# One bank, one copy for two pairs of f tiles, and eight 64-row products in one stay: the first MLP layer of an FNet block

## The chip, the core and the metric

The kernel runs on one core of a Trainium2 chip. A core has a matrix engine (TensorE; PE in the profile, its weight loads PEld), a vector engine (DVE), a scalar engine (ACT), GpSimd (POOL) and a queue engine (SP) that here only issues transfers. Each takes its instructions in the order written into the program. Matmuls write PSUM, eight banks of 128 partitions by 512 fp32; DVE and ACT copy from there to SBUF. The metric is the time of one execution on the device in microseconds: the median of three runs before the change is 1242.02 (1241.27 to 1242.12).

## The reference, cut to what matters

x is 2048 tokens by 576 features; w1 is 576x4608, w2 is 4608x576.

```python
xn = _layernorm(x)
a = einsum("bsd,ed->bse", xn, dft_hid_re); b = einsum("bsd,ed->bse", xn, dft_hid_im)
y = einsum("ts,bse->bte", dft_seq_re, a) - einsum("ts,bse->bte", dft_seq_im, b)
h = maximum(einsum("bsd,df->bsf", xn, w1), 0)
return x + y + einsum("bsf,fd->bsd", h, w2)
```

## The kernel before, in words

**Numbers.** Every operand is split into a high and a low float16 part, and a product of two operands is three matmuls: high by high, high by low, low by high. Most products are those of a scheme with seven half-size products in place of eight (`PRODUCTS` for the second layer and the sequence DFT, `P1` to `P7` for the first layer).

**The loops.** The 4608 hidden features are nine blocks b of 512, and the tokens four groups g of 512. A *step* is one (b, g). In it the first layer makes the hidden values `h` of this step, and the second layer (`mlp2`, seven products m0 to m6 of twelve matmuls 128x288 each) works on the `h` of the step before. After the 36 steps come the hidden DFT (`dft1`) and the sequence DFT.

**The first layer from block 2 on** (`BB = 2`, 28 steps; blocks 0 and 1 do it with whole products in `mlp1_step`). A block has two *pairs* of f tiles of 128 (index i). For each pair `pair_products` makes seven products P1, P2, P6, P5, P7, P3, P4 on 256 tokens: six matmuls 128x256 each (two blocks of 128 features, three matmuls for each), written into half of a bank (256 columns of 512). 576 features are four blocks of 128 and a *rest* of 64. The rest enters with four of the products (`REST`): each has two more matmuls, one with the high weights and one with the low weights. In the 128 rows of both operands the 64 rest rows stand twice: in the weights the same rows again, in the tokens (`xT[g][:, KM]`) high and then low part. So the matmul with the low weights adds low by high and, with its other 64 rows, low by low. A pair's step is thus 50 matmuls, both pairs' 100.

**Banks and copies.** Four banks: one `u` for each pair, and `v`, `w` for both. P1 is copied out of `u` (ACT), then P6 adds onto it in PSUM, is copied (ACT), then P7 (DVE), then P4. P2 goes to `v`; P5 and then P3 to `w`. Each product that adds onto a bank must wait until the copy before has read it. The copies and the arithmetic on the values (`free`, `use`, `end_s`) are 128x256 for each pair. At the end `end_hi` (ACT) and `end_lo` (DVE), 128x1024 each, make high and low part of the four sums S1 to S4 of a pair; they stand in the list `ends`, which later places in the order take from.

**The order of the work** is written by hand: the list of `(do, q)` from L1075 on. In it `first` and `second` issue the products of the two pairs, `m` the second layer's, `later1` and `later2` the arithmetic on values, `ready` and `brief` one piece each of the preparation of the next block (loads, maxima, scales, `split_w1b`, `sums_w1`, `split_w2`), `t_sum` sums of token operands, and `count` one piece of the sequence DFT's scales: `sum_c` sums a loaded 128x1024 tile `f` on ACT (L1027), then `first_c` asks for the next one over SP (L1020) into the same buffer. So each `f` has the time from one `count` to the next to land, and ACT stands until it has. There are two `count`s a step.

**What m0 to m6 need.** Two PSUM tiles serve them. m0, m2, m4, m6 add onto one place, m1 has one for itself, m3 and m5 share the third; m0, m2, m3, m6 are copied out by ACT (L612), m1, m4, m5 merged by DVE (L616), and m1, m4, m5, m6 are then added to memory by a POOL transfer (`spill`, L619). m3 takes the buffer that m1 leaves, and m6 adds onto what m4's merge has read.

**64-row matmuls** stand already in `mlp1_step` (L371) and `dft1` (L1203): there the low products of the rest use only 64 rows each, in turns rows 0 to 63 and rows 64 to 127 of the array; for the second kind `xT[g][:, NKX]` holds the high part in rows 64 to 127.

The launch lays the inputs out on the host.

Of the kernel before, what the change touches and what calls it, by code (L numbers as in the profile page):

```python
# [9 lines left out]
F16 = mybir.dt.float16  # L10
# [8 lines left out]
P = 128  # L19
S = 2048  # L20
D = 576
# [28 lines left out]
def kernel(  # L50
# [35 lines left out]
    accs = [accp.tile([P, TG, D], F32, name=f"acc{g}") for g in range(NG)]  # L86
# [6 lines left out]
    raws = {}  # L93

# [9 lines left out]
    def load_w1(b, i, parts=1):  # L104
        pool, tag = (raw, "raw") if b else (mlp, "stage")
        r = raws["w1", b, i] = pool.tile([P, 2 * KT, P], F32, tag=tag, name=f"raw_w1_{b}_{i}")
# [271 lines left out]

    def mlp1_out(b, g, i, pa, pb, after=None, last=None, late=False):
# [5 lines left out]
        h = hs[b, g, i] = mlp.tile([P, 2, 7, GH], F16, tag="h", name=f"h{b}_{g}_{i}", bufs=4)  # L385
        st = mlp.tile([P, 5, GH], F32, tag="stage", name=f"s{b}_{g}_{i}")
# [5 lines left out]
        for q, src in ((slice(A11, A11 + 1), a11), (slice(A12, A22 + 1), pb)):  # L392
            hi, lo = (h[:, n, q].rearrange("p a b -> p (a b)") for n in range(2))
            with behind(after):
                order["hi"] = nc.scalar.activation(hi, src, AF.Relu).ins
                order["hl"] = stt(lo, src, 0.0, hi, ALU.max, ALU.subtract).ins  # L396
# [33 lines left out]
    flat = [a.rearrange("p a b -> p (a b)") for a in accs]  # L430
    XS = 4 * 2 * (KM // 2) * GH // 2
    xsums = [
        f[:, : XS].bitcast(F16).rearrange("p (q n k t) -> p q n k t", q=4, n=2, t=GH)
        for f in flat
    ]
    cbufs = [f[:, XS :] for f in flat]
# [59 lines left out]
    banks1, ends, gates = [], [], {}  # L496

    def freed(i, key="free"):

        order[key] = i.ins  # L500

    def pair_products(b, g, i):

        if not banks1:
            banks1.extend(ps1.tile([P, G], F32, tag="ps1", name=f"bank{k}")[:, :GH] for k in range(4))
        h = hs[b, g, i] = mlp.tile([P, 2, 7, GH], F16, tag="h", name=f"h{b}_{g}_{i}", bufs=4)
        st = mlp.tile([P, 5, GH], F32, tag="stage", name=f"s{b}_{g}_{i}")
        r21, s1, s2, s3, s4 = (st[:, n] for n in range(5))
# [4 lines left out]
        def product(n):  # L513
            ps = {P2: v, P5: w, P3: w}.get(n, u)
            first = n in (P1, P2, P5)
            x, ws, a = right(g, n), w1s[b, i], LEFT[n]
            todo = [
                (ws[:, y, a + k], x[z][:, k]) for k in range(2) for y, z in ((1, 0), (0, 0), (0, 1))
            ]
            if n in REST:  # L520
                k, c = REST[n]
                todo += [(ws[:, y, k], xT[g][:, KM, (H1, H2)[c]]) for y in range(2)]
            for m, (l, r) in enumerate(todo):
                nc.tensor.matmul(  # L524
                    ps, l, r, start=first and m == 0, stop=m == len(todo) - 1,
                    skip_group_check=not first,
                )
# [6 lines left out]
        def end_s():  # L534
# [3 lines left out]
            stt(s4, u, 0.0, s2, ALU.max, ALU.subtract)  # L538

        hi_s, lo_s = (h[:, k, S1 : S4 + 1] for k in range(2))  # L540

        def end_hi():
            order["s"] = nc.scalar.activation(hi_s, st[:, 1:], AF.Copy).ins  # L543

        def end_lo():
            order["lo"] = nc.vector.tensor_tensor(lo_s, st[:, 1:], hi_s, ALU.subtract).ins  # L546

# [4 lines left out]
            P6: lambda: freed(nc.scalar.activation(s1, u, AF.Copy)),  # L552
            P5: lambda: freed(nc.scalar.activation(c22, w, AF.Copy)),
            P7: lambda: freed(tt(c22, u, c22, ALU.add), "vfree"),  # L554
            P3: lambda: freed(tt(r21, w, s1, ALU.add), "vfree"),
# [4 lines left out]
            P3: lambda: nc.scalar.activation(r21, r21, AF.Relu),  # L560
            P4: lambda: (value(A12, u), end_s(), ends.extend((end_hi, end_lo))),
        }

        def run(n, used=False):
            if used:
                return use[n]()
            product(n)
            if n in free:
                free[n]()

        return run
# [109 lines left out]
    def sum_w2(b, i, after=("root", 4)):  # L681
# [3 lines left out]
        if b:  # L685
            junk = mlp.tile([P, 5, GH], F32, tag="stage", name=f"j{b}_{i}")
            junk = junk.rearrange("p a b -> p (a b)")[:, : 4 * EH]
            junk = junk.rearrange("p (q e) -> p q e", e=EH)
        else:
            new_w2(b, i)  # L690
            junk = w2s[b, i][:, 0, :4]
# [41 lines left out]
    def split_w2(b, i, c):  # L733
        if b and c == 0:
            new_w2(b, i)
# [247 lines left out]
    def split_d(j, c):  # L983
        k = PARTS_D[c]
        split(dsp[j][:, 0, k], dsp[j][:, 1, k], raws["d", j][:, k], sc["d"][:, j : j + 1])
# [52 lines left out]
    for n in range(2, len(steps)):  # L1038
# [26 lines left out]
        if b >= BB:  # L1065
            first, second = (pair_products(b, g, i) for i in range(NQ))
            later1, later2 = (lambda q, f=f: f(q, True) for f in (first, second))
# [6 lines left out]
            t_sum = lambda q: next(tq, None)  # L1074
            for do, q in (  # L1075
                (first, P1), (first, P2), (m, 0), (left, 0), (end, 0), (first, P6),
                (brief, 1), (first, P5), (end, 0), (later1, P2), (m, 1), (left, 1),
                (t_sum, 0), (ready, 1), (second, P1), (first, P7), (ready, 1), (m, 2),
                (second, P2), (t_sum, 0), (count, 0), (brief, 1), (first, P3), (first, P4), (later1, P7), (m, 3),
                (second, P6), (later1, P3), (later1, P4), (later2, P2), (brief, 1), (m, 4),  # L1080
                (t_sum, 0), (second, P5), (ready, 1), (m, 5), (end, 0), (second, P7),
                (t_sum, 0), (end, 0), (brief, 1), (m, 6), (count, 0), (brief, 2),
                (second, P3), (second, P4), (later2, P7), (later2, P3), (later2, P4), (brief, 1),
            ):
                do(q)
# [304 lines left out]
```

## Time and profile before

| what | value |
|---|---|
| median of three runs | 1242.02 us |
| profiled execution, first to last instruction | 1239.7 us |
| PE busy | 1226.7 us (99%), 10269 matmuls |
| DVE busy | 1006.8 us (81%), 1919 instructions |
| ACT busy | 704.1 us (57%), 1192 instructions |
| POOL busy | 159.9 us (13%) |
| TensorE clock granted | 1.000 |
| stretch of the 28 steps with `pair_products` | 192.4 to 788.1 us |

The profile's own execution has a span of 1239.7 us, 2.3 us under the median of the runs, which time the launch and the end as well. Busy time of PE is an envelope: matmuls overlap in the pipeline, a row's mean duration (273 ns for 256 columns) is the latency of one, and the distance from one start to the next is shorter. A line such as `L524 PE MATMUL bank<-acc,w1buf 128*128 128x256 f16 x768` names line, engine, operation, output and inputs, the array's rows and columns in use, the output's shape, and the count; then come busy time and mean ns, then the engine's idle time just before and what ended it.

### The profile page before, as it was taken

Reading aid. Unit: us, or ns where it says so; the run is one execution under the profiler, and the core shown is the slowest. Engines: PE = TensorE matmul, PEld = TensorE weight load, DVE = VectorE, ACT = ScalarE, POOL = GpSimd, SP = SyncE. Lnnn points to the kernel's source line nnn. Section 1 sums busy time; section 2 is a strip of 40 time slices with the busy share of each in tenths; the row PEclk is TensorE's granted clock in tenths of the full one; section 3 lists DMA queues with packets and bytes.
Section 4 is the critical chain, followed back from the end, with each engine's and each line's share of the span. In section 5 each row is a group of like instructions: output and inputs, shape, how many; then the busy total and the mean of one; then the engine's idle time right before and its main releaser. Section 6 shows DMA issues by size and latency. Waiting matters only on the chain.

```text
span 1239.7 us, 25267 instructions
## 1 busy us (share of the span) xinstructions
PE 1226.7 (99%) x10269; PEld 980.6 (79%) x10269; DVE 1006.8 (81%) x1919; ACT 704.1 (57%) x1192; POOL 159.9 (13%) x208
## 2 busy tenths in 40 slices
PE   8999999999999999999999999999999999999998
PEld 7656657888888888888888888777777777777776
DVE  8999999878778788788787788466887878787875
ACT  5655566666676776766766666445543333333332
POOL 2432212121111112121212111200000000000000
PEclk9999999999999999999999999999999999999999
DMA  8995537556666766676676766720054344434420
GB/s 313 210 163 97 85 68 153 127 119 151 140 136 141 137 143 121 135 140 137 112 172 122 158 141 123 127 71 1 1 174 141 122 125 138 142 120 129 134 88 20
DMA packets 80324, 157.28 MB, mean 127 GB/s; under 512 B 22224, under 2 KB 41168, under 8 KB 80208
## 3 DMA queue, kind: packets, MB, share of 16 engines
q1 hardware_dynamic: 57424, 113.20, 28.7%
q0 software_dynamic: 22784, 42.48, 25.8%
q8 instruction: 80, 1.31, 0.4%
q14 instruction: 36, 0.29, 0.1%
HBM read 104.53 MB, written 51.90 MB: 126 GB/s over the span
## 4 chain that ended last, share of the span: by engine, by line
PE 92%; DVE 5%; ACT 1%; issue 1%; DMA 0%; SPq 0%; ACTq 0%; DVEq 0%
PE p L601 28%; PE p L1322 27%; PE bank L524 23%; PE pd L1193 8%; PE p L346 5%; DVE w2s L186 1%; DVE st L209 1%; DMA acc<-in_x_dram 0%; PE pd L1203 0%; DVE h L413 0%; DVE dbuf L260 0%; ACT f L1027 0%; DVE w1buf L186 0%; ACT h L543 0%; DVE h L396 0%
## 5 line engine op out<-in xcount | busy, mean ns | idle before, releaser
L601 PE MATMUL p<-w2s,h 128*128 128x288 f16 x3024 | 408.0, 286 | 1.5 <-DVE acc L616 0.8
L601 PEld LDWEIGHTS <-h 128*128 128x128 f16 x3024 | 295.6, 98 | 76.9 <-issue 1.7
L1322 PE MATMUL p<-R,cs 128*128 128x288 f16 x2688 | 329.4, 286 | 0.0
L1322 PEld LDWEIGHTS <-cs 128*128 128x128 f16 x2688 | 263.0, 98 | 66.3
L185 ACT ACTIVATE cs<-c,sc_c 128x1024 f16<-128x1024 f32 x112 | 125.2, 1144 | 196.7 <-DVE c L1255 72.3
L186 DVE SCALAR_TENSOR_TENSOR cs<-c,sc_c,cs 128x1024 f16<-128x1024 f32 x112 | 141.0, 1281 | 54.7 <-ACT cs L185 54.7
L524 PEld LDWEIGHTS <-w1buf 128*128 128x128 f16 x1600 | 156.6, 98 | 21.9 <-issue 0.7
L524 PEld LDWEIGHTS <-dbuf 128*128 128x128 f16 x1200 | 117.4, 98 | 16.1 <-issue 0.3
L524 PE MATMUL bank<-xT,w1buf 128*128 128x256 f16 x832 | 109.9, 273 | 0.0
L1193 PE MATMUL pd<-dbuf,xT 128*128 128x288 f16 x832 | 103.8, 286 | 0.0
L524 PE MATMUL bank<-acc,w1buf 128*128 128x256 f16 x768 | 102.3, 273 | 0.4 <-ACT acc L550 0.2
L546 DVE TENSOR_TENSOR h<-s,h 128x1024 f16<-128x1024 f32 x56 | 68.5, 1223 | 38.4 <-ACT h L543 38.4
L1193 PEld LDWEIGHTS <-xT 128*128 128x128 f16 x832 | 80.8, 98 | 22.0 <-issue 1.9
L619 POOL DMA_DIRECT2D spill<-dbuf x70 | 60.5, 865 | 252.7 <-DVE dbuf L616 229.7
L531 ACT ACTIVATE h<-acc 128x256 f16<-128x256 f32 x112 | 45.8, 411 | 67.3 <-DVE acc L554 66.5
L524 PE MATMUL bank<-xT,dbuf 128*128 128x256 f16 x624 | 82.3, 273 | 0.0
L543 ACT ACTIVATE h<-s 128x1024 f16<-128x1024 f32 x56 | 59.1, 1056 | 33.8 <-DVE s L538 33.5
L524 PE MATMUL bank<-acc,dbuf 128*128 128x256 f16 x576 | 76.6, 273 | 0.1
L1328 DVE SCALAR_TENSOR_TENSOR o<-p,us_c,o 128x288 f32<-128x288 f32 x112 | 57.5, 513 | 12.7 <-PE p L1322 12.0
L612 ACT ACTIVATE dbuf<-p,c_ub 128x576 f32<-128x576 f32 x70 | 51.4, 734 | 26.4 <-PE p L601 26.3
L1027 ACT ACTIVATE f<-f 128x1024 f32<-128x1024 f32 x60 | 62.8, 1046 | 0.3 <-DMA f<-in_cre_dram 0.3
L619 POOL DMA_DIRECT2D spill<-sum x42 | 36.9, 878 | 196.1 <-DVE sum L616 173.4
(164 smaller groups left out, 1529.4 us busy)
## 6 DMA issues: line engine op xcount, KB each, us to landing
spill<-dbuf POOLq DMA_DIRECT2D x70, 288.0 KB, 5.0
c<-in_cre_dram SPq DMA_DIRECT2D x32, 512.0 KB, 4.1
c<-in_cim_dram SPq DMA_DIRECT2D x32, 512.0 KB, 5.0
f<-in_cre_dram SPq DMA_DIRECT2D x30, 512.0 KB, 6.0
f<-in_cim_dram SPq DMA_DIRECT2D x30, 512.0 KB, 5.7
spill<-sum POOLq DMA_DIRECT2D x42, 288.0 KB, 4.4
raw_w<-in_w_dram SPq DMA_DIRECT2D x17, 640.0 KB, 5.2
raw_w<-in_w_dram SPq DMA_DIRECT2D x18, 576.0 KB, 4.9
```

The costliest lines, as they stand in the source:

```text
L185: nc.scalar.activation(hi, src, AF.Copy, scale=s).ins,
L186: nc.vector.scalar_tensor_tensor(lo, src, s, hi, ALU.mult, ALU.subtract).ins,
L346: order["m1"] = nc.tensor.matmul(ps[:, cols], w1s[b, i // 2][:, hl, i % 2 * KT + k], xT[g][:, kx, cols], start=(start and n == 0), stop=(s ...
L524: nc.tensor.matmul(ps, l, r, start=first and m == 0, stop=m == len(todo) - 1, skip_group_check=not first,)
L543: order["s"] = nc.scalar.activation(hi_s, st[:, 1:], AF.Copy).ins
L546: order["lo"] = nc.vector.tensor_tensor(lo_s, st[:, 1:], hi_s, ALU.subtract).ins
L601: order["pe"] = nc.tensor.matmul(ps[:, c], h[:, x, qa, c * P : (c + 1) * P], w[:, y, qb], start=first and i == 0 and j == 0, stop=i == NQ ...
L619: nc.gpsimd.dma_start(spill[g, row, col], o, accum_op=ALU.add)
L1027: nc.scalar.activation(f, f, AF.Abs, scale=2.0**-10, accum_out=sums_c[:, n, q : q + 1])
L1193: nc.tensor.matmul(ps[j], xT[g][:, kx, c * P : (c + 1) * P], dsp[j][:, hl, k], start=(t % 2 == 0 and n == 0), stop=(t % 2 == 1 and n == le ...
L1322: nc.tensor.matmul(ps, w[:, a, k], r[:, c, rq], start=first and k == 0 and j == 0, stop=k == HK - 1 and j == 2, skip_group_check=not first,)
L1328: order["o"] = nc.vector.scalar_tensor_tensor(o, ps, us["c"][:, n : n + 1], o, ALU.mult, ALU.add).ins
```

## The change

From block 2 on, `step_products(n)` replaces the two `pair_products`.

- **Shared banks.** `u` is one bank for both pairs, each in its half; `v` likewise; P5 and P3 use `w`, which is in turn bank 2 and bank 3 from step to step. A product is issued for pair 0 and then pair 1, and then one copy of 128x512 reads both. `h` is one tile for both pairs, `stage` one tile for the whole kernel, and the four `acc` tiles become one (`acct`) so that `cbufs` are two buffers of 128x512. P4 is now copied out by ACT (`s4`), and A12 and S4 are made from that copy.
- **Rest.** P2, P5, P3 and P4 keep their matmul with the high weights. The eight matmuls with the low weights (four products, two pairs) are taken out and become 64-row matmuls that stand together in `rests`, between m3 and P3: P4's and P3's of this step, and P2's and P5's of the *next* step (they open the next step's `v` and `w`). They go in turns to rows 0 to 63 and 64 to 127 of the array. The low by low part of the rest is no longer added. The first of the 28 steps does its P2 and P5 lows in the old way, and the last has only four in `rests`.
- **Order.** The list of `(do, q)` is new: P1, P5, m0, P6, P2, m1, P7, m2, m3, `rests`, P3, m4, P4, m5, m6. The two `count`s come after m2 and after m5.
- **Smaller edits.** `end_hi` and `end_lo` cover two sums of both pairs, still 128x1024, and two of them follow each of m0 and m1 in the tail. `split_w1b` and `split_d` are queued behind the latest copies out of the banks. `sum_w2` writes its unused result into the `w2s` tile of the next block, not into a `stage` buffer.

```diff
-    accs = [accp.tile([P, TG, D], F32, name=f"acc{g}") for g in range(NG)]
+    acct = accp.tile([P, NG, TG, D], F32, name="acc")
+    accs = [acct[:, g] for g in range(NG)]
...
+    stage = mlp.tile([P, 5, NQ, GH], F32, name="stage", bufs=1)
...
+    def new_h(b, g, i):
+        if i == 0:
+            h = mlp.tile([P, 2, 7, NQ, GH], F16, tag="h", name=f"h{b}_{g}")
+            for j in range(NQ):
+                hs[b, g, j] = h[:, :, :, j]
+            hs[b, g] = h
+        return hs[b, g, i]
...
-    def pair_products(b, g, i):
+    def step_products(n):
+        b, g = steps[n]
...
-        u, v, w = banks1[i], banks1[2], banks1[3]
-        c11, c22 = cbufs[i], cbufs[2]
+        u, v, w = banks1[0], banks1[1], banks1[2 + n % 2]
+        c11, c22 = cbufs
...
+        def product(q):
+            ps = {P2: v, P5: w, P3: w}.get(q, u)
+            x, a = right(g, q), LEFT[q]
+            first = q in (P1, P2, P5) and (n, q) not in begun
+            for i in range(NQ):
+                ws = w1s[b, i]
+                todo = [
+                    (ws[:, y, a + k], x[z][:, k]) for k in range(2) for y, z in ((1, 0), (0, 0), (0, 1))
+                ]
+                if q in REST:
+                    k, c = REST[q]
+                    lows = q in (P2, P5) and (n, q) not in begun
+                    todo += [(ws[:, y, k], xT[g][:, KM, (H1, H2)[c]]) for y in range(1 + lows)]
+                for m, (l, r) in enumerate(todo):
+                    nc.tensor.matmul(
+                        ps[:, i], l, r, start=first and i == m == 0,
+                        stop=m == len(todo) - 1, skip_group_check=not first or i > 0,
+                    )
+
+        def rests(also=None):
+            todo = []
+            if also is not None:
+                b2, g2 = steps[also]
+                for i in range(NQ):
+                    todo += [(banks1[1], b2, g2, i, P2, i == 0), (banks1[2 + also % 2], b2, g2, i, P5, i == 0)]
+                begun.update(((also, P2), (also, P5)))
+            for i in range(NQ):
+                todo += [(u, b, g, i, P4, False), (w, b, g, i, P3, False)]
+            for m, (ps, b_, g_, i, q, start) in enumerate(todo):
+                r, kx = m % 2, (KM, NKX)[m % 2]
+                rows = slice(r * REM, (r + 1) * REM)
+                k, c = REST[q]
+                nc.tensor.matmul(
+                    ps[:, i], w1s[b_, i][rows, 1, k], xT[g_][rows, kx, (H1, H2)[c]],
+                    start=start, stop=True, skip_group_check=not start,
+                )
...
+        def end_hi(i):
+            with behind("free"):
+                order["s"] = nc.scalar.activation(h[:, 0, S1 + 2 * i :][:, :2], stage[:, 1 + 2 * i :][:, :2], AF.Copy).ins
...
+        def sums_h():
+            nc.scalar.activation(r21, r21, AF.Relu)
             stt(s3, c11, 0.0, r21, ALU.max, ALU.subtract)
             stt(s1, c22, 0.0, r21, ALU.max, ALU.add)
             stt(s2, c22, 0.0, s3, ALU.max, ALU.subtract)
...
+        def last():
+            hi, lo = h[:, 0, A12], h[:, 1, A12]
+            nc.scalar.activation(hi, s4, AF.Copy)
+            tt(lo, s4, hi, ALU.subtract)
+            tt(s4, s4, s2, ALU.subtract)
+            for i in range(NQ):
+                ends.extend((lambda i=i: end_hi(i), lambda i=i: end_lo(i)))
...
+            P4: lambda: freed(nc.scalar.activation(s4, u, AF.Relu)),
...
-        split(w[:, 0, k], w[:, 1, k], src, sc["w1", b][:, i : i + 1])
+        with behind("free"), behind("vfree"):
+            split(w[:, 0, k], w[:, 1, k], src, sc["w1", b][:, i : i + 1])
...
+        new_w2(b, i)
+        junk = w2s[b, i][:, 0, :4]
...
             for do, q in (
-                (first, P1), (first, P2), (m, 0), (left, 0), (end, 0), (first, P6),
-                (brief, 1), (first, P5), (end, 0), (later1, P2), (m, 1), (left, 1),
-                (t_sum, 0), (ready, 1), (second, P1), (first, P7), (ready, 1), (m, 2),
-                (second, P2), (t_sum, 0), (count, 0), (brief, 1), (first, P3), (first, P4), (later1, P7), (m, 3),
-                (second, P6), (later1, P3), (later1, P4), (later2, P2), (brief, 1), (m, 4),
-                (t_sum, 0), (second, P5), (ready, 1), (m, 5), (end, 0), (second, P7),
-                (t_sum, 0), (end, 0), (brief, 1), (m, 6), (count, 0), (brief, 2),
-                (second, P3), (second, P4), (later2, P7), (later2, P3), (later2, P4), (brief, 1),
+                (run, P1), (left, 0), (run, P5), (end, 0), (end, 0), (m, 0), (brief, 1), (left, 1),
+                (run, P6), (end, 0), (end, 0), (run, P2), (t_sum, 0), (m, 1), (used, P2), (ready, 1),
+                (run, P7), (t_sum, 0), (ready, 1), (m, 2), (used, P7), (count, 0), (m, 3), (brief, 1),
+                (rest, 0), (run, P3), (brief, 1), (m, 4), (used, P3), (t_sum, 0), (ready, 1),
+                (run, P4), (used, P4), (t_sum, 0), (m, 5), (ready, 1), (count, 0),
+                (m, 6), (brief, 3),
             ):
...
-        if ends:
-            ends.pop(0)()
+        for _ in range(2):
+            if ends:
+                ends.pop(0)()
```

More of the change, by code (lines that the diff above doesn't have):

```diff
@@ L391, in mlp1_out @@
             nc.scalar.activation(r21, a21, AF.Relu)
-        for q, src in ((slice(A11, A11 + 1), a11), (slice(A12, A22 + 1), pb)):
-            hi, lo = (h[:, n, q].rearrange("p a b -> p (a b)") for n in range(2))
+        both = pb.rearrange("p (a t) -> p a t", t=GH)
+        for q, src in ((A11, a11), (slice(A12, A22 + 1), both)):
+            hi, lo = (h[:, n, q] for n in range(2))
             with behind(after):
@@ L537, in end_s @@
             stt(s2, c22, 0.0, s3, ALU.max, ALU.subtract)
[L538 to L546, printed above, removed]
+        def last():
[3 more added lines that the diff above has]
+            tt(s4, s4, s2, ALU.subtract)
+            for i in range(NQ):
+                ends.extend((lambda i=i: end_hi(i), lambda i=i: end_lo(i)))
         free = {
@@ L1065 @@
         if b >= BB:
-            first, second = (pair_products(b, g, i) for i in range(NQ))
-            later1, later2 = (lambda q, f=f: f(q, True) for f in (first, second))
+            run, rests = step_products(n)
+            used = lambda q: run(q, True)
             m = lambda q: mlp2(pb, pg, q)
```

87 lines of the change are left out of this document (41 added, 46 removed).

## The prediction

> **What bounds the kernel now.** First the page's engine totals, its clock row and the chain that ended last.
>
> ```profile
> PE 1226.7 (99%) x10269; PEld 980.6 (79%) x10269; DVE 1006.8 (81%) x1919; ACT 704.1 (57%) x1192; POOL 159.9 (13%) x208
> ...
> PEclk9999999999999999999999999999999999999999
> ...
> PE 92%; DVE 5%; ACT 1%; issue 1%; DMA 0%; SPq 0%; ACTq 0%; DVEq 0%
> PE p L601 28%; PE p L1322 27%; PE bank L524 23%; PE pd L1193 8%; PE p L346 5%; DVE w2s L186 1%; DVE st L209 1%; DMA acc<-in_x_dram 0%; PE pd L1203 0%; DVE h L413 0%; DVE dbuf L260 0%; ACT f L1027 0%; DVE w1buf L186 0%; ACT h L543 0%; DVE h L396 0%
> ```
>
> PE is the bound at full clock. Only fewer PE slots or fewer PE waits shorten the time; DVE and ACT count where they keep PE waiting. Then the busy times of the stretch of the 28 changed steps and of one step in it.
>
> ```profile
> 192.00:795.00 603.00, 601.87 (x5211) 509.47 (x5210) 489.67 (x1076) 408.69 (x800) 106.43 (x136) 1.00 0.66 137
> 384.80:406.03 21.23, 21.23 (x187) 18.02 (x186) 18.05 (x40) 13.97 (x29) 3.82 (x6) 1.00 0.65 132
> ```
>
> Columns after the length: PE, PEld, DVE, ACT, POOL. A step is 21.23 us without a gap; in all 603 us PE lacks 603.00 - 601.87 = 1.13 us. So nothing is to be had from waits: at most 1.1. But DVE has 18.05 of 21.23 us, so a merge that is wanted earlier may come late.
>
> **The low products.** From PE's timeline, slots of full-height matmuls and three places where 64-row ones stand already.
>
> ```profile
> 387.81 1.47 PE L524 MATMUL bank<-acc,w1buf 128*128 128x256 f16 x12
> 389.12 0.38 PE L524 MATMUL bank<-xT,w1buf 128*128 128x256 f16 x2
> 389.34 1.63 PE L601 MATMUL p<-w2s,h 128*128 128x288 f16 x12
> 390.81 0.82 PE L524 MATMUL bank<-xT,w1buf 128*128 128x256 f16 x6
> ...
> 392.12 1.63 PE L601 MATMUL p<-w2s,h 128*128 128x288 f16 x12
> 393.59 1.91 PE L524 MATMUL bank<-xT,w1buf 128*128 128x256 f16 x16
> ...
> 396.21 1.02 PE L601 MATMUL p<-w2s,h 128*128 128x288 f16 x7
> ...
> 804.23 1.27 PE L1193 MATMUL pd<-dbuf,xT 128*128 128x288 f16 x9
> 805.43 0.67 PE L1203 MATMUL pd<-dbuf,xT 64*128 64x288 f16 x8
> 806.02 0.79 PE L1193 MATMUL pd<-dbuf,xT 128*128 128x288 f16 x5
> ...
> 109.78 0.61 PE L371 MATMUL p<-xT,dbuf 64*128 64x512 f16 x4
> 110.31 1.04 PE L346 MATMUL p<-xT,dbuf 128*128 128x512 f16 x4
> ```
>
> Slot of 256 columns: (389.12 - 387.81) / 12 = 0.109 us. Of 288: (390.81 - 389.34) / 12 = 0.1225. A stay of eight 64-row matmuls: nine full ones from 804.23 would hand over at 804.23 + 9 x 0.1225 = 805.33; the stay begins at 805.43 (0.10 late) and lasts 0.59, where eight in turn would need 0.98 and four pairs side by side 0.49. So they run in pairs, and a stay costs about 0.10 going in and 0.10 coming out; 0.21 with the two next starts (from the starts of single matmuls). L371 agrees: 0.53 for four of 512 columns, two slots of 0.216 and 0.10.
>
> A middle step: eight slots go (0.874), four slots and a stay come (0.437 + 0.21 = 0.65): -0.224. Of 28 steps 26 are such: -5.83. The first keeps four lows in full slots: +0.21. The last has two pair slots in place of eight: -0.44. Sum A = **-6.06**.
>
> The Trainium skill ("TensorE: Matmul & The Clock Gate", section Part 3: Packing small matmuls) puts a pack at one matmul and about 4 ns more for each tile, with no price for the stay. By it a step would save 0.42 us, 28 some 11.8, and the run would take 1230. Its sister page ("TensorEngine Tiling (Array Packing)", Key Properties) says that changing the tiling mode drains the engine; the 0.21 us above agree, and the sum goes by the row.
>
> **The copies.** These are the forms that change or that stand in the way (mean ns in the middle).
>
> ```profile
> L395 ACT ACTIVATE h<-p 128x512 f16<-128x512 f32 x16 | 9.4, 591 | 18.1 <-PE p L346 17.8 <-DVE h L396 0.3
> L396 DVE SCALAR_TENSOR_TENSOR h<-p,h 128x512 f16<-128x512 f32 x16 | 10.8, 678 | 0.0
> L531 ACT ACTIVATE h<-bank 128x256 f16<-128x256 f32 x56 | 20.7, 370 | 0.2 <-PE bank L524 0.2
> L551 DVE TENSOR_TENSOR acc<-bank,acc 128x256 f32<-128x256 f32 x56 | 23.3, 416 | 3.1 <-PE bank L524 3.1
> L543 ACT ACTIVATE h<-s 128x1024 f16<-128x1024 f32 x56 | 59.1, 1056 | 33.8 <-DVE s L538 33.5
> L546 DVE TENSOR_TENSOR h<-s,h 128x1024 f16<-128x1024 f32 x56 | 68.5, 1223 | 38.4 <-ACT h L543 38.4
> L612 ACT ACTIVATE dbuf<-p,c_ub 128x576 f32<-128x576 f32 x70 | 51.4, 734 | 26.4 <-PE p L601 26.3
> L616 DVE SCALAR_TENSOR_TENSOR dbuf<-p,c_ub,dbuf 128x576 f32<-128x576 f32 x56 | 45.4, 812 | 6.5 <-PE p L601 6.1
> L185 ACT ACTIVATE w1buf<-raw_w,c_sw 128x640 f16<-128x640 f32 x20 | 16.3, 824 | 4.7 <-DVE c_sw L127 3.6 <-DVE raw_w L678 1.0
> L1027 ACT ACTIVATE f<-f 128x1024 f32<-128x1024 f32 x60 | 62.8, 1046 | 0.3 <-DMA f<-in_cre_dram 0.3
> ```
>
> Ten DVE instructions of 0.416 for each pair become ten of 0.68 for both: 1.5 us a step less by durations. ACT has seven of 0.37 to 0.41 for each pair and gets eight of about 0.6: 0.6 less. Both stay beside PE and earn nothing; the bound is 0 to -1.13, and the waits there are now are booked below.
>
> What PE has to wait for, in its new order (P1 1.31, P5 1.53, m0 1.47, P6 1.31, P2 1.53, m1 1.47, P7 1.31, m2 1.47, m3 1.47, rests 0.65, P3 1.53, m4 1.47, P4 1.53, m5 1.47, m6 1.47; sum 21.0):
> - P6 after P1's copy (ACT): 1.53 + 1.47 = 3.0 us for 0.59. P7 after P6's: the same. Next P1 after P4's copy: 2.9.
> - P4's lows after P7's add (DVE, 0.68): 2.94 and two pair slots, 3.2.
> - m3 after m1's merge (DVE, 0.81): 1.31 + 1.47 = **2.78**, where the rows above give 396.21 - 390.81 = 5.40 today. m6 after m4's merge: 1.53 + 1.47 = 3.0.
> - m2 after the sums' low part: 5.7 and more, easy.
>
> How late a merge is today, in the same step:
>
> ```profile
> 391.98 0.81 DVE L616 SCALAR_TENSOR_TENSOR sum<-p,c_ub,sum 128x576 f32<-128x576 f32 x1
> ```
>
> m1's merge ends at 392.79, 1.98 after m1's slots. In 2.78 that fits, with 0.8 over. By the order of the built program I added up a plain step of the changed kernel in the same way: DVE reaches P2's add at 8.7 us of the step (splits and sums of w1 to 5.3, S's two low parts 1.22 each, the second after ACT's at 7.45), ends m1's merge at 10.2 against m3 at 11.4, and P7's add, behind a split of 0.88, at 12.5 against 13.1. So a plain step has 1.2 and 0.6 us over: no wait.
>
> New waits, where that fails:
> - First of the 28 steps: ahead of P7's add DVE has P2's add, four sums of token operands, m1's merge, A11's low part and a w2 split, some 6.8 us where PE needs 6.05: 0.7.
> - Last step: the DFT scale is known 3.0 us into it, then ACT splits 1.0 and 0.77, then copies P1 (0.6): 5.2 against P6 at 4.3: 0.9.
> - Tail: S's parts now all follow m0's copy: 0.7 + 1.06 on ACT against m1's 1.47: 0.3.
> - Steps of blocks 0 and 1: their arithmetic is reordered among itself by a few instructions, PE's order is the same: 0 to 0.6, taken 0.3.
> - Late `f`. ACT comes to the second `count` some 4.5 us after the first has asked for its `f` (first `count` ends at 14.4 of the step, P4's copy at 18.9). If `f` is not there, ACT stands, and behind it A12's high part, then on DVE its low part, the weights' scale (a POOL reduction and three small instructions), ACT's split, DVE's sums, P2's add and m1's merge. That chain has the 1.2 us over. So PE waits when `f` takes more than about 5.7 us.
>
> How long `f` takes, over all 60, and for the one asked for at 385.1 (by the second `count` today) and at 395.9 (by the first):
>
> ```profile
> DMA to landing us min/median/max: 3.3/5.8/8.4
> ...
> L1020 SPq DMA_DIRECT2D f<-in_cre_dram x1: 327/327/327, 385.1 to 385.1; - x1
> ...
> DMA to landing us min/median/max: 7.0/7.0/7.0
> ...
> L1020 SPq DMA_DIRECT2D f<-in_cim_dram x1: 328/328/328, 395.9 to 395.9; - x1
> ...
> DMA to landing us min/median/max: 4.8/4.8/4.8
> ```
>
> The two kinds alternate: the slow one is asked for among the spills of m5 and m6, the fast one between those of m1 and m4. In the new order the first `count`'s still falls between them (m1's spill starts at 10.2, m4's at 17.3), and the slow one gets over 12 us. So mostly 3.5 to 5, no wait; above 5.7 where a weight load of 576 KB stands beside it, in two or three blocks: four waits of 0.5 to 0.75, 2.4 us. On SP the loads of w2 queue behind `f` and wait with it; on POOL the reduction stands between spills and adds nothing more. Bounds for all this: 0, and at 7 us for every first `f` half a microsecond or more in 28 steps, 14.
>
> Sum C = 0.7 + 0.9 + 0.3 + 0.3 + 2.4 = **+4.6**. Today's waits go: **B = -1.1**. Other edits: `sum_w2` into the w2s tile needs m6 of the block before, done a step earlier: 0; one transfer and POOL instruction count is unchanged.
>
> A + B + C = -6.06 - 1.1 + 4.6 = -2.6. The profiled execution: 1239.7 - 2.6 = 1237.1; the runs' median stands 2.3 above: 1242.0 - 2.6 = **1239.4**. Now 0.2% (2.5 us) is about what a measurement of this kernel can tell from no change, and the forecast lies on that edge.
>
> **The rivals.**
> - *All hidden*: `f` lands in under 5.7 us everywhere and DVE keeps up. For it: PE lacks 1.1 us in 603 today. Against: 2.78 where 5.40 was. A + B and a little: 1235 to 1236.
> - *Late `f`* (the other side): one mechanism, ACT held at the second `count`. For it: the median of 5.8 and the 7.0; today ACT stood 0.3 us for it in all. Against: the fast kind. It decides from about 5.7 us for the typical first `f`: at 6.2, 0.3 us in 28 steps, 1245; at 7, 1252. Between, it eats the gain: 1240 to 1244.
> - *Not side by side*: eight serial slots and a stay: +0.21 x 28 = 5.9, 1248. Against it stands the 0.59 us.
> - *No price for the stay*: 0.437 in 28 steps, -12, 1230. Against it stand 0.10 and 0.10. The span model of the Trainium skill, above, is this one.
>
> **How the numbers follow.** The forecast (some waits, 1237.5 to 1241.5) 0.45, of that 0.25 below 1239.5; all hidden 0.19; no price for the stay 0.01; late `f` 0.31, of that 0.13 inside 0.2% and 0.18 above 1244.5; not side by side 0.04. Faster 0.25 + 0.19 + 0.01 = 0.45; same 0.20 + 0.13 = 0.33; slower 0.18 + 0.04 = 0.22. The range from 1235 (all hidden) to 1246 (a first `f` of 6.2) leaves out not quite 2 in 10.
>
> **What the next profile would show.** Right: a middle step of 21.0 us; a stay of eight 64x256 matmuls of some 0.54 us between starts; ACT's idle time before `f` a few microseconds where it was 0.3; PE waits of 3 to 5 us in the stretch, most on DVE merges. Wrong: steps over 21.5 us, ACT's wait for `f` of tens of microseconds, P4's lows waiting for P7's add in every step, or a stay that costs other than 0.21.

## The result and the profile after

The changed kernel takes 1239.42 us (median of 20 runs, 1237.31 to 1240.61) against 1241.85 (1240.91 to 1242.76) beside it: ratio 0.9979, 95% interval 0.9972 to 0.9986. That is 2.4 us less, by the interval 1.7 to 3.5. The forecast was 1239.4. Three executions far outside the rest, two of the kernel before beside the experiments (4591 us) and one of run 7 (2135 us, at a granted clock of 0.56), stand in no ratio here. The profiled execution has a span of 1236.6 us against 1239.7, both at a granted clock of 1.000.

Engine totals and the chain that ended last, from the page of the changed kernel:

```profile
PE 1221.1 (99%) x10269; PEld 965.6 (78%) x10269; DVE 988.3 (80%) x1639; ACT 696.1 (56%) x1024; POOL 158.8 (13%) x208
...
PE 78%; DVE 11%; issue 5%; DMA 2%; ACT 2%; POOL 1%; SPq 0%; POOLq 0%; ACTq 0%; DVEq 0%
```

DVE has 280 instructions and 18.5 us less, ACT 168 and 8.0 less, and PE is busy 99% as before. But the chain was 92% PE and is 78%: a piece of it now runs over DVE, ACT and a transfer. Busy times of the changed stretch and of one plain step (length, PE, PEld, DVE, ACT, POOL):

```profile
192.00:790.00 598.00, 594.99 (x5206) 493.53 (x5205) 472.54 (x799) 400.99 (x632) 107.08 (x137) 1.00 0.64 137
460.88:481.86 20.98, 20.98 (x186) 17.44 (x186) 17.59 (x31) 14.06 (x23) 3.80 (x5) 1.00 0.63 114
```

The plain step went from 21.23 to 20.98 us, still without a gap. The stretch lacks 598.00 - 594.99 = 3.0 us where 1.1 was lacking. PE's timeline of one stay (the 64-row matmuls that stand together), and then all of PE's waits from 100 us on (us in total, times, longest):

```profile
393.55 3.10 PE L665 MATMUL p<-w2s,h 128*128 128x288 f16 x24
396.59 0.61 PE L578 MATMUL bank<-xT,w1buf 64*128 64x256 f16 x8
397.13 1.05 PE L559 MATMUL bank<-xT,w1buf 128*128 128x256 f16 x8
```

```profile
PE p L665 <- DVE acc L680: 1.9, 1, 1.9
PE bank L578 <- DVE acc L615: 1.0, 1, 1.0
PE bank L559 <- ACT acc L611: 0.8, 1, 0.8
PE p L665 <- ACT sums L676: 0.7, 1, 0.7
PE p L665 <- DVE sum L680: 0.5, 1, 0.5
PE p L665 <- DVE dbuf L680: 0.4, 1, 0.4
PE p L665 <- ACT h L590: 0.2, 1, 0.2
```

24 slots of 0.1225 from 393.55 end at 396.49, the stay begins 0.10 later and the next full matmul starts 0.54 after it: four pair slots and 0.10. That is the price that was forecast. The first wait in the list, of 1.9 us, stands at 115 us, ahead of the stretch.

These rows count a wait from the modelled end of the matmul before. From here on a wait is counted from start to start: the distance to the start before, less the slots between. So of m3's wait in block 4,

```profile
414.58 1.63 PE L665 MATMUL p<-w2s,h 128*128 128x288 f16 x12
416.65 1.63 PE L665 MATMUL p<-w2s,h 128*128 128x288 f16 x12 [0.44 <-DVE dbuf L680]
```

the row says 0.44, and by starts it is 416.65 - 414.58 - 12 x 0.1225 = 0.60. By that count PE waited, between the first product of the stretch and the end of the hidden DFT, 2.30 us in the kernel before (eight waits of up to 0.43) and 4.65 in the changed one: 1.16 in the first of the 28 steps (at 207.96), 0.60 and 0.67 in block 4 (416.65, 425.44), 0.98 in the last step (767.95), 0.41 and 0.83 in the tail (788.00, 794.59). The difference of the two spans splits like this:

| piece | us |
|---|---|
| first product of the stretch, 192.56 to 193.17 | +0.61 |
| from there to the last `dft1` matmul, 713.82 to 710.19 | -3.63 |
| of that: waits, 2.30 to 4.65 | +2.35 |
| of that: slots, the rest | -5.98 |
| after it | -0.10 |
| span | -3.12 |

So the slots gave what they were said to give (A was -6.06), and 2.4 us of them came back as waits. The experiments ask whether the slots are the whole gain, where the waits come from, and whether they must be.

### The profile page after: what moved, and what is told of

It reads as the page before. It is cut to its first block, busy times and chain, and to the rows that moved or that the text cites. A ratio compares the mean times of both kernels' runs of the same rounds, so it can differ in the third digit from the quotient of the medians.

```text
span 1236.6 us, 24680 instructions
## 1 busy us (share of the span) xinstructions
PE 1221.1 (99%) x10269; PEld 965.6 (78%) x10269; DVE 988.3 (80%) x1639; ACT 696.1 (56%) x1024; POOL 158.8 (13%) x208
## 4 chain that ended last, share of the span: by engine, by line
PE 78%; DVE 11%; issue 5%; DMA 2%; ACT 2%; POOL 1%; SPq 0%; POOLq 0%; ACTq 0%; DVEq 0%
PE p L1381 27%; PE p L665 21%; PE bank L559 19%; PE pd L1252 8%; PE p L356 1%; PE bank L578 1%; DVE h L431 1%; DVE w2s L196 1%; DMA raw_w<-in_w_dram 1%; POOL spill L683 1%; DVE w1buf L196 1%; DMA spill<-sums 1%; DVE h L414 1%; DVE st L219 1%; DVE acc L491 1%
## 5 line engine op out<-in xcount | busy, mean ns | idle before, releaser
L665 PE MATMUL p<-w2s,h 128*128 128x288 f16 x3024 | 399.1, 286 | 4.7 <-DVE acc L680 2.7
L559 PEld LDWEIGHTS <-w1buf 128*128 128x128 f16 x1476 | 143.0, 98 | 22.5 <-issue 4.4
L559 PEld LDWEIGHTS <-dbuf 128*128 128x128 f16 x1104 | 107.0, 98 | 16.1 <-issue 2.5
L594 DVE TENSOR_TENSOR h<-stage,h 128x1024 f16<-128x1024 f32 x56 | 68.4, 1223 | 42.2 <-ACT h L590 42.2
L559 PE MATMUL bank<-acc,w1buf 128*128 128x256 f16 x768 | 97.8, 273 | 0.8 <-ACT acc L611 0.8
L559 PE MATMUL bank<-xT,w1buf 128*128 128x256 f16 x708 | 95.8, 273 | 0.0
L585 ACT ACTIVATE h<-acc 128x512 f16<-128x512 f32 x56 | 35.2, 629 | 75.8 <-DVE acc L615 40.0
L559 PE MATMUL bank<-acc,dbuf 128*128 128x256 f16 x576 | 73.3, 273 | 0.0
L559 PE MATMUL bank<-xT,dbuf 128*128 128x256 f16 x528 | 71.5, 273 | 0.0
L590 ACT ACTIVATE h<-stage 128x1024 f16<-128x1024 f32 x56 | 58.7, 1050 | 0.0
```

The lines of the kernel that those rows point to most:

```text
L559: nc.tensor.matmul(ps[:, i], l, r, start=first and i == m == 0, stop=m == len(todo) - 1, skip_group_check=not first or i > 0,)
L590: order["s"] = nc.scalar.activation(h[:, 0, S1 + 2 * i :][:, :2], stage[:, 1 + 2 * i :][:, :2], AF.Copy).ins
L594: order["lo"] = nc.vector.tensor_tensor(lo, stage[:, 1 + 2 * i :][:, :2], hi, ALU.subtract).ins
L665: order["pe"] = nc.tensor.matmul(ps[:, c], h[:, x, qa, c * P : (c + 1) * P], w[:, y, qb], start=first and i == 0 and j == 0, stop=i == NQ ...
```

## The experiments

Each is an edit of the changed kernel, 8 and 9 on top of other runs' edits. The ratios stand to the kernel before, which ran beside each.

**1. The low products in full slots again.**

```diff
-                    lows = q in (P2, P5) and (n, q) not in begun
+                    lows = 1
...
-                (rest, 0), (run, P3), (brief, 1), ...
+                (run, P3), (brief, 1), ...
```

> All eight low products go back to full-height slots behind their high ones and the stay of 64-row matmuls is gone; shared banks, wide copies and order stay. Theory (the gain is the products' alone, term A): 8 slots of 0.109 us come back for 4 slots and 0.21 us, 26 x 0.224 + 0.44 - 0.21 = +6.06 us, less up to 1 us because P4's lows no longer stand 0.4 us behind m3 and wait 1.2 us for P7's add in the first step: 1244.4 to 1245.5. It is then slower than the kernel before by the new waits, 2.5 to 3.6 us. Rival (wide copies and fewer instructions carry the gain): under 1241.

Measured: 1242.25 us, ratio 1.0002 (0.9993 to 1.0011): the time of the kernel before. From the first product to the last `dft1` matmul it takes 713.74 us where before took 713.82, and its waits there are 2.26 against 2.30. PE's waits from 192 us on:

```profile
PE p L665 <- DVE dbuf L680: 0.7, 2, 0.4
PE p L665 <- DVE sum L680: 0.2, 1, 0.2
```

The rival falls: shared banks, wide copies, the new order and some 450 instructions fewer, taken together, earn nothing that shows. (One of the smaller edits costs time, as runs 8 to 10 show; what each part is worth alone was not measured.) The theory is right on the slots and misses the time by 2 to 3 us: with the eight full slots back in each step the waits fall by 2.4, from 4.65 to 2.26, where 1 at most was expected. The slots came back: 713.74 - 710.19 + 2.39 = 5.94 us. In these two profiles, then, half of the changed kernel's waits goes when PE is slower again.

**2. All low products on one half of the array.**

```diff
-                r, kx = m % 2, (KM, NKX)[m % 2]
+                r, kx = 0, KM
```

> All eight low products of a step use rows 0 to 63 of the array; the stay, its place and the order stay. Theory (products on different halves run side by side): four more slots of 0.109 us in 27 steps and two more in the last, 27 x 0.437 + 0.22 = +12.0 us, 1251.4, and a stay of 0.54 us becomes one of about 0.98. Rival (they never ran side by side, the gain is from fewer rows loaded): no change, 1239.4.

Measured: 1248.95 us, ratio 1.0059 (1.0045 to 1.0073). A stay in its timeline:

```profile
400.72 1.04 PE L578 MATMUL bank<-xT,w1buf 64*128 64x256 f16 x8
```

1.04 against 0.61: the eight run in turn. From first product to last `dft1` matmul it takes 10.22 us more than the changed kernel with 1.60 less of waits, so the slots cost 11.8 where 12.0 was expected. The time stays 2.4 us under the expected 1251.4, mostly for these waits. In the changed kernel two matmuls on different halves start 3 to 4 ns apart. So they do run side by side.

**3. Two stays a step.**

```diff
-            rest = lambda q: rests(n + 1 if n + 1 < len(steps) else None)
+            rest = lambda q: rests() if q else n + 1 < len(steps) and rests(n + 1, False)
...
-                ... (count, 0), (m, 3), (brief, 1), (rest, 0), (run, P3), ...
+                ... (count, 0), (rest, 0), (m, 3), (brief, 1), (rest, 1), (run, P3), ...
```

(`rests(n, False)` issues only the next step's products, `rests()` only this step's.)

> The eight low products stand in two stays of four instead of one of eight: those of the next step's P2 and P5 ahead of m3, those of P4 and P3 behind m3 as they are. Same matmuls, same slots. Theory (each stay costs about 0.10 us going in and 0.10 coming out, however long it is): 27 more stays x 0.21 = +5.7 us, less 0.2 us of the first step's wait, some 1244.9. Rival (a stay has no price of its own): 1239.2.

Measured: 1244.65 us, ratio 1.0021 (1.0012 to 1.0031): slower than the kernel before, and where the theory had it. The two stays of a step:

```profile
461.52 1.63 PE L665 MATMUL p<-w2s,h 128*128 128x288 f16 x12
463.08 0.39 PE L578 MATMUL bank<-xT,dbuf 64*128 64x256 f16 x4
463.41 1.64 PE L665 MATMUL p<-w2s,h 128*128 128x288 f16 x12
464.99 0.39 PE L578 MATMUL bank<-xT,dbuf 64*128 64x256 f16 x4
465.31 1.70 PE L559 MATMUL bank<-xT,dbuf 128*128 128x256 f16 x14
```

461.52 + 12 x 0.1225 = 462.99: 0.09 late. From 463.08 to 463.41 are 0.33 for two pair slots of 0.109: 0.11 more. The second stay shows the same. By starts the 27 stays cost 5.05 + 0.61 of saved waits = 5.66 us, 0.21 each, whether four matmuls stand in one or eight. Two stays take back 0.42 of the 0.437 us that a step's pairs save; gathering all eight in one is what leaves something.

**4. `f` in time.** Every `f` lands early; ACT's sum of it stays.

```diff
-        f = firsts[m] = mlp.tile([P, HK, P], F32, tag="first", ..., bufs=1)
+        if m == 4:
+            firsts["f"] = mlp.tile([P, HK, P], F32, tag="first", ..., bufs=1)
+        f = firsts[m] = firsts["f"]
+        k = slice(0, HK if m == 4 else 1)
...
-            nc.sync.dma_start(f, blocks_c(n)[q])
+            nc.sync.dma_start(f[:, k], blocks_c(n)[q][:, k])
...
-                f, f, AF.Abs, scale=2.0**-10, ...
+                f, f, AF.Abs, scale=2.0**-7, ...
```

> One buffer f stays for the whole kernel, and each load after the first brings an eighth of it (64 KB instead of 512 KB); ACT's sum over the whole 128x1024 stays. Left out: the scales of the sequence DFT come from an eighth of its matrix, times eight. So f is there early in every step. Theory (the waits of block 4 come from the order of DVE's queue and not from f): the waits of about 0.6 and 0.7 us in block 4 stay, ACT's 3 us before f go, the time stays within 0.5 us of 1239.4. Rival (the term of 2.4 us for a late f, as forecast): these waits go and the time falls by 1 to 2.4 us to 1237.0 to 1238.4.

Measured: 1238.67 us, ratio 0.9977 (0.9966 to 0.9988), which cannot be told from the changed kernel's 0.9979. The time lies between the two forecasts, 0.2 us below the theory's and 0.3 above the rival's, so the profiles have to decide. In the changed kernel these rows say how long ACT waited for `f` (us, times) and how long `f` took to land:

```profile
  DMA f<-in_cre_dram: 1.8, 1
  DMA f<-in_cim_dram: 1.1, 2
```

```profile
DMA to landing us min/median/max: 3.3/4.9/11.3
```

In this run ACT has no such idle time, and from first product to last `dft1` matmul it takes 710.29 us where the changed kernel took 710.19. PE in its block 4:

```profile
418.37 1.63 PE L665 MATMUL p<-w2s,h 128*128 128x288 f16 x12 [0.44 <-DVE dbuf L680]
427.15 1.63 PE L665 MATMUL p<-w2s,h 128*128 128x288 f16 x12 [0.51 <-DVE sum L680]
```

The changed kernel's rows for these two have 0.44 and 0.51 as well. They are not `f`'s. What stands ahead of m1's merge, which m3 waits for, is DVE's queue; in the changed kernel's block 4:

```profile
408.53 0.15 DVE L137 TENSOR_SCALAR c_sw<-half 128x1 int32<-128x1 int32 x1
...
409.58 0.88 DVE L196 SCALAR_TENSOR_TENSOR dbuf<-raw_w,c_sw,dbuf 128x640 f16<-128x640 f32 x1 [0.83 <-ACT dbuf L195]
...
414.06 1.22 DVE L594 TENSOR_TENSOR h<-stage,h 128x1024 f16<-128x1024 f32 x1
415.19 0.68 DVE L612 TENSOR_TENSOR acc<-bank,acc 128x512 f32<-128x512 f32 x1
415.79 0.81 DVE L680 SCALAR_TENSOR_TENSOR dbuf<-p,c_ub,dbuf 128x576 f32<-128x576 f32 x1
```

The step began at 404.66; a weight scale known 3.9 us into it, two splits, sums and S's second low part come before P2's add and m1's merge, which ends at 416.60 where m3 wants it at 416.05.

**5. That phase, one block later.**

```diff
-        ... ((2, 2) if b < BB else (3 + (b == BB), 0)))
+        ... ((2, 2) if b < BB else (3 + (b == BB) + (b == 5), 0)))
```

> One empty piece more in the list that prepares block 5, so that its pieces fall one place later in the hand-written order; no engine gets more or less work. Theory (block 4's two waits come from the one place in which the weights' maximum, scale and splits stand on DVE ahead of P2's add and m1's merge): both waits, about 0.6 and 0.7 us on merges, leave block 4 (416 and 425 us) and turn up in block 5, some 84 us later (500 and 509); time as it was, 1239.4. Rival (something in block 4 itself, a late load or f): they stay at 416 and 425.

Measured: 1239.46 us, ratio 0.9982 (0.9972 to 0.9992). No wait is left at 416 to 427, and two stand in the next block:

```profile
501.70 1.63 PE L665 MATMUL p<-w2s,h 128*128 128x288 f16 x12 [0.44 <-DVE dbuf L680]
510.48 1.63 PE L665 MATMUL p<-w2s,h 128*128 128x288 f16 x12 [0.51 <-DVE sum L680]
```

The waits move with the phase and keep their size, 0.60 and 0.67 by starts. The list of a block has 39 pieces for 40 places, so each block starts one place earlier than the one before until none is left over; only one of these phases puts the scale where it hurts.

**6. `f` late.** A quarter of it is loaded again behind it.

```diff
             nc.sync.dma_start(f, blocks_c(n)[q])
+            if m > 4:
+                nc.sync.dma_start(f[:, :2], blocks_c(n)[q][:, :2])
```

> Each f after the first is followed by a second transfer of its first quarter into the same buffer, which must wait for the first; so f is complete some 2 to 3 us later than in the changed kernel (median 4.9 us there), at 7 to 8 us. Theory (the chain from a late f as forecast: ACT held at the second count, then A12's parts, the scale, the sums, P2's add and m1's merge, with PE waiting from 5.7 us on): 1.3 to 2.3 us in each of 28 steps, +36 to +64 us, 1275 to 1303. Rival (the slack is larger than that sum, or only one of two f's comes in time to matter): ACT stands tens of microseconds before f, and the time rises by less than 14 us.

Measured: 1272.53 us (two runs), ratio 1.0249 (1.0231 to 1.0267), under the 1275 to 1303 of the theory and far over the rival's. What ACT waited for at its sums (us, times), how long the second transfer took, and what PE waited for most:

```profile
  DMA f<-in_cre_dram: 39.4, 13
  DMA f<-in_cim_dram: 37.5, 16
```

```profile
DMA to landing us min/median/max: 2.3/2.9/5.7
```

```profile
PE bank L559 <- ACT acc L611: 19.4, 9, 3.6
PE p L665 <- DVE dbuf L680: 3.1, 5, 1.1
```

The chain that was forecast is real: about one `f` a step makes ACT stand, 76.9 us in all, and PE takes 32.4 us more from first product to last `dft1` matmul. It is priced too high: 4.7 us for `f` (median in this run) and 2.9 for the second transfer are 7.6, which is 1.9 over the 5.7 of the forecast, and 28 x 1.9 = 53. Most of it reaches PE at another place than forecast, by P1's copy on ACT (L611), and less by the merges. And some 3.3 of the 32.4 us are no waits: after PE's two longest, 3.74 and 3.60 us by starts (ending at 686.87 and 755.53), a slot of 256 columns takes 0.213 us instead of 0.109 for some 3.4 us each, at a granted clock of 0.50. After its three waits of 2.8 to 3.0 us in the stretch the clock stayed at 1.00.

**7. The waits taken away by order.**

```diff
-        ... ((2, 2) if b < BB else (3 + (b == BB), 0)))
+        ... ((2, 2) if b < BB else (3 + (b == BB) - (b == 5), 0)))
...
-                    todo += [lambda: None, lambda d=d: later(d)]
+                    todo += [lambda: None] * (1 + 2 * (j == 3)) + [lambda d=d: later(d)]
...
-                    for _ in range((2, 0, 0, 5, 0, 0, 2)[q]):
+                    for _ in range((2, 0, 0, 6, 0, 0, 2)[q]):
...
-            for _ in range(1 + i % 2 if b else (2, 2, 2, 4)[i]):
+            for _ in range(1 + i % 2 + 3 * (n == 4 and i == 1) if b else (2, 2, 2, 1)[i]):
...
-                o = sumbufs[sum_buffer(g, n)]
+                o = sumbufs[3 if (b, g, n) == (NB - 1, NG - 1, 3) else sum_buffer(g, n)]
```

In the tail (m0 to m6 of the last step, behind the loop) the two `ends` are taken ahead of each product, not shown above; `sumbufs[3]` is the old `sum0`, free by then.

> The waits of the changed kernel taken away by order alone: the token sums end one step earlier (first step, 1.16 us), one empty piece less ahead of block 5 (block 4, 1.32), two empty pieces more ahead of the last DFT scale (last step, 0.98), S's parts ahead of m0 in the tail and m3's copy there into a free buffer (0.41 and 0.83), three pieces of block 1's weights later (of 2.0 us at 113 us some 0.7). Same instructions on every engine. Theory (these waits are all that C cost): 4.7 + 0.7 = -5.4 us against the changed kernel, span 1231.2, time 1234.0. Rival (what is freed is late next, half of it comes back): 1236 to 1237.

Measured: 1236.84 us, ratio 0.9962 (0.9949 to 0.9975), with a profiled execution of 1233.64 (span 1231.9). From its profile the waits that were aimed at are gone, of the 2.02 us at 115 us 0.61 are left, and one is new, in the tail:

```profile
785.99 0.74 ACT L676 ACTIVATE sums<-p,c_ub 128x576 f32<-128x576 f32 x1 [2.98 <-DMA spill<-sums]
...
786.79 4.57 PE L665 MATMUL p<-w2s,h 128*128 128x288 f16 x36 [1.16 <-ACT sums L676]
```

m2's copy waits for the transfer that still reads its buffer. The profiled execution agrees with the theory, the median with the rival: four others took 1236.3 to 1237.6, and this profile does not show why.

**8. Run 7 with three buffers of their own for the last step's m2, m3 and m6.**

```diff
+            w = mlp.tile([P, 2, 7, EH], F16, tag="w2s", name="more", bufs=4)
+            w = w.rearrange("p n q e -> p (n q e)").bitcast(F32)
+            sumbufs.extend(
+                w[:, k : k + 2 * EH].rearrange("p (c e) -> p c e", e=EH)
+                for k in range(0, 6 * EH, 2 * EH)
+            )
...
-                o = sumbufs[sum_buffer(g, n)]
+                o = sumbufs[{2: 3, 3: 4, 6: 5}.get(n, 1) if (b, g) == (NB - 1, NG - 1) else sum_buffer(g, n)]
```

> As the run before it, but the last step's m2, m3 and m6 are copied into three buffers of their own (a free w2s tile), because the copy of m2 there stood 2.98 us for the transfer that still read its buffer, and PE 1.33 us behind it. Theory (a buffer held by a spill, not ACT, made m4 wait in the tail): that wait goes, span 1230.6 in the profile, and 1.3 us less than the run before in the time, 1235.5. Rival (the copy is late for ACT's own queue): the wait of 1.3 us stays, 1236.8.

Measured: 1234.85 us, ratio 0.9946 (0.9932 to 0.9959). No wait is left in the tail, as the theory had it, and first product to last `dft1` matmul takes 706.41. But the span is 1233.1 instead of 1230.6, for this profile caught what the last one missed. On ACT and PE, ahead of the stretch:

```profile
178.36 1.16 ACT L753 ACTIVATE w2s<-raw_w 128x1152 f16<-128x1152 f32 x1 [4.37 <-DMA raw_w<-in_w_dram]
...
179.53 0.72 ACT L676 ACTIVATE sum<-p,c_ub 128x576 f32<-128x576 f32 x1
```

```profile
180.30 3.10 PE L665 MATMUL p<-w2s,h 128*128 128x288 f16 x24 [1.95 <-ACT sum L676]
```

ACT stands 4.37 us for block 2's second w2 load, m0's copy behind it, and PE 2.1 us for that (and 0.93 more in the first step, at 206 us). By starts this wait of PE was 0 in the profiles of the changed kernel and of runs 2, 5 and 7, 0.26 in run 1, 0.54 in run 3, 0.68 in run 4 and 1.18 in run 6. The kernel before has none. The split that reads its buffer, and the load as it was asked for, in the kernel before and then in the changed one:

```profile
166.53 0.87 DVE L186 SCALAR_TENSOR_TENSOR w1buf<-raw_w,c_sw,w1buf 128x640 f16<-128x640 f32 x1
...
167.43 0.33 SPq L100 DMA_DIRECT2D raw_w<-in_w_dram  x1
```

```profile
170.42 1.54 DVE L196 SCALAR_TENSOR_TENSOR w1buf<-raw_w,c_sw,w1buf 128x640 f16<-128x640 f32 x2
...
172.03 0.33 SPq L107 DMA_DIRECT2D raw_w<-in_w_dram  x1
```

The load needs the raw buffer that w1's last split of the block reads, and that split on DVE is now the second of two from 170.42 on. One of the "smaller edits" moved it: `split_w1b` is queued behind the latest copies. The chain of the changed kernel leads from there into the stretch (start, us, what):

```profile
170.50 1.47 DVE w1buf L196 x2
172.03 5.35 DMA raw_w<-in_w_dram
...
187.54 1.13 DVE w2s L196
...
206.58 0.73 DVE w2s L196
207.31 0.61 DVE acc L615
207.96 0.40 PE bank L578 x4
```

By this chain the first step's wait of 1.16 hangs on this load too: late load, late w2 scale, and a w2 split ahead of P7's add.

**10 and 9. That edit undone: in the changed kernel (run 10), and in run 8's, the one without the waits (run 9).**

```diff
-        with behind("free"), behind("vfree"):
+        with behind("free" if b > BB else None), behind("vfree" if b > BB else None):
             split(w[:, 0, k], w[:, 1, k], src, sc["w1", b][:, i : i + 1])
```

> The changed kernel with one of its smaller edits undone: block 2's w1 splits are no longer queued behind the latest copies out of the banks. Theory (that edit lets the last split of block 2 end at 172 us instead of 167, the load of w2 into the same raw buffer is asked for at 172.0 instead of 167.4, ACT stands 1 to 4 us for it, and the copy of m0 behind it makes PE wait 0 to 2 us, another amount in each execution): the load is asked for before 170, ACT's wait for it goes, and PE's wait at 180 us; the time falls by 0.3 to 1.3 us to 1238.1 to 1239.1, and the runs lie closer together than 3.3 us. Rival (splits ahead of the hidden values' copies cost more than they give): PE waits in blocks 0 and 1 grow, 1239.4 to 1241.

> The same edit undone in the kernel without the waits (1234.85, where its profile shows ACT 4.4 us idle for this load, PE 2.1 us behind it at 180 us and 0.9 at 205 us). Theory: both waits of PE go, -2.5 us on its profile (span 1230.6), 1232.5 in time. Rival: within 0.5 us of 1234.85.

Measured: in the changed kernel (run 10) 1236.69 us, ratio 0.9963 (0.9950 to 0.9975), five runs from 1236.3 to 1237.9. The load and ACT's sum there:

```profile
167.90 0.33 SPq L107 DMA_DIRECT2D raw_w<-in_w_dram  x1
```

```profile
174.19 1.15 ACT L753 ACTIVATE w2s<-raw_w 128x1152 f16<-128x1152 f32 x1
```

ACT's wait for the load is gone, PE has none at 180 us, and the first step's 1.16 us at 208 are gone too. By the medians that is 2.7 us less for one line, where 0.3 to 1.3 was forecast; the two intervals still touch. The profile accounts for about 1 us of it: from first product to last `dft1` matmul it takes 709.21 us, 0.98 less. Where the rest lies it does not show. It has another wait, 0.58 at 661, with ACT 1.88 us idle for an `f` until 656.65: a late `f` can strike in some executions.

In the kernel without the waits (run 9) 1232.63 us, ratio 0.9934 (0.9921 to 0.9948), span 1230.9, as the theory had it: no wait over 0.3 us is left from 192 us to the end of the tail, and the 2.02 us at 115 us are 0.73. The load there is asked for only at 170.63, ACT still stands 1.56 us, and PE does not notice. This version beats both kernels, the one before by 8.9 us.

## Why the prediction was right, and where it was not

The median of 1239.42 against a forecast of 1239.4 is luck to that last digit: the term for a late `f` (2.4 us) was wrong and B was off by 1.2 us, and what stood in their place nearly made up for it. Term by term:

- **A, the slots (-6.06)**: right. -5.98 in the profiles, 5.94 by run 1, pairs side by side by run 2, 0.21 us for a stay by run 3. With this the rivals "not side by side" and "no price for the stay" fall. The pack model of the Trainium skill's "TensorE: Matmul & The Clock Gate" (Part 3) has no term for what run 3 measures. The Trainium skill's "TensorEngine Tiling (Array Packing)" (Key Properties), by which a change of mode drains the engine, gives no size; the 0.09 in and 0.11 out of run 3 agree with it.
- **Copies at nothing**: right. Run 1 has them and no pairs, and takes the time of the kernel before. The 1.5 us a step that DVE was to be spared were 0.7 (18.5 us in all): I had added up durations, but these instructions overlap, and 0.416 and 0.68 us long they start 0.335 and 0.60 apart. DVE is not the bound, so it changed nothing.
- **B, the waits of the kernel before (-1.1)**: mis-sized. The page's busy time hid half of them: by starts there were 2.30 us.
- **First step (0.7) and last step (0.9)**: 1.16 and 0.98, at the places and from the releasers named. But the first one's cause was only half seen: the w2 split ahead of P7's add stood there because its load was late (run 10 takes the wait away without touching the step).
- **Tail (0.3)**: 0.41 came as forecast, another 0.83 from a copy that waits for a spill of the step before, which no term held. It is not in every execution: in the profiles of runs 1 to 5 and 10 PE loses at most 0.17 there.
- **Early blocks (0.3)**: the first product came 0.61 later in the profile; in the six other profiles with the same early code (runs 1 to 6) it came at 193.26 to 194.51, 0.70 to 1.95 later. So 0.3 was too little in all seven, but the kernel before has one profile alone, and part of it is the late load of the last item. A wait of some 2 us at 115 us (1.73 to 2.03) is in all seven and not in the kernel before, while a wait of 1.49 at 85 us is only there.
- **Late `f` (2.4)**: this step failed. `f` landed in 4.9 us by the median instead of 5.8, ACT stood 2.9 us for it in all (1.8 of them after the tail), and no wait of PE in the profile came from it (run 4). In its place stand 1.27 us in block 4 from the order on DVE. The 1.2 and 0.6 us that a plain step was to have over are there in one (in the step from 468.90 m1's merge and P7's add end 1.45 and 1.2 us early); but I had added up one phase of the preparation and taken it for all, and the phase of block 4 does not fit. For that reason the waits on merges are only these 1.27 us of the 4.65, where I had announced most of them there. The two prices for a later `f` did not fit each other either: with 1.2 us over, an `f` of 7 us would cost 28 x 1.3 = 36 us and not the 14 given; run 6, at some 7.6, cost 32.4.
- **"Other edits: 0"**: this failed too. Queueing `split_w1b` behind the copies put off a load on SP by 4.6 us; ACT waited for it with a PSUM copy behind. It is the mechanism of the late `f` with another load, just ahead of the stretch where I had looked. At that place it costs PE nothing to 2.1 us from one profile to the next.

C came out at 4.65 in the stretch and tail and 0.61 ahead of them, 5.3 where 4.6 stood, and B at -2.3 where -1.1 stood: -5.98 - 2.30 + 5.26 = -3.0 for the -2.6 of the forecast. The sum held because B and C were both too small and partly cancel, and because the term for a late `f` happened to be as large as waits of other causes.

## What to carry to other kernels

When PE is the bound and its slots get fewer, add up not only a plain step but the first, the last, the tail and every phase in which hand-placed pieces can fall: there the other engines' lateness appears, and in run 7 moving one list of pieces by one place was enough to take 1.3 us of waits away. When a piece is queued later, follow the buffer that it frees to the load that waits for it and to the engine that will stand for that load. Pairs of 64-row matmuls pay 0.21 us for each stay and not for each pair, so gather them.

## What the runs showed of the hardware beside that

The same load of 576 KB, asked for at 172.0 in the changed kernel's profile and at 170.5 in run 8's, landed after 5.4 us there and 7.9 here, and PE's wait behind it went from 0 to 2.1 us; the changed kernel's runs spread over 3.3 us where those of the kernel before spread over 1.9. That this load is the whole spread was not shown: with the edit undone the runs spread over 1.6 and 2.5 us, but over five runs only.
